# Moving the routing marks to GpSimd and reordering the routing inside a fused attention and mixture-of-experts kernel

## The chip, the cores and the metric

The kernel runs on one core of a Trainium2 chip. The metric is the device time of one execution in microseconds (us). The core's engines run side by side, each through its own queue in the order in which it was written: TensorE (PE in the profile; PEld is its weight load), VectorE (DVE), ScalarE (ACT), GpSimd (POOL) and SyncE (SP, which only issues transfers). Semaphores tie them together.

## The reference, cut to what matters

Sliding-window attention (4 batches, 8 heads, 576 positions, width 64, window 64) gives 2304 tokens of 512 columns. A router with noise picks two of eight experts for each token and weighs them; each expert is two matrix products with a ReLU between. The sum goes through a last feed-forward block (2048 columns, a piecewise quadratic gate).

```python
scores = np.where((rel >= 0) & (rel < 64), q @ k.T / 8, -1e9)
x = softmax(scores) @ v                               # 2304 x 512
noisy = x @ w_gate + np.log1p(np.exp(x @ w_noise)) * noise
top2, top2_w = two largest of noisy, softmax over the two
out[t] = sum over the two: top2_w * (np.maximum(x[t] @ w1[e], 0) @ w2[e])
return gate(out @ w_in) @ w_out                       # w_in, w_out come as float64
```

## The kernel before

**Stages.** The first stage is attention, in half-steps `step(u)`, u = 0 to 36. A tile is 128 tokens; two half-steps, an even and an odd one, carry one tile through a pipeline of several tiles at once. An even step does the scores of the tile ahead (`A`, L282 and L291), transposes an older output tile (`Ex`, L347), transposes probabilities (`C`, L313), and multiplies them with the values (`Dm`, L327). An odd step has `C` and the router's logits (`logits`, `Gm`, L365). ScalarE does the exponentials (L306) and copies out of PSUM (L315, L349); VectorE does the maxima (L298), the normalised values (L332, L333, L335) and copies the logits (L368). GpSimd scales the maxima (L299) and copies 64 value rows per tile (L340) that the next tile's `Dm` reads.

**Routing.** The 18 tiles form three groups of six (`GROUPS`). When a group's last logits are there, `route(g)` is made, a generator. Every step calls `advance(marks)`, which lets it go on to its next `yield` of 1 or 2 (`yield 0` does not stop it), and then lets up to `marks` queued calls run. In order, the generator computes the noisy logits, the two largest and their indices (L454, L457), one-hot rows and their sums (L460 to L478), then the positions of the tokens within their experts as matrix products (L482 to L486), their split in row and column (L491 to L505), and queues 12 calls (6 tiles, 2 choices), each `mark_r` and `mark_e`. A mark is a 128x128 (`ohr`, L510) or 128x145 (`ohe`, L517, for odd tiles of a group; L520 on ScalarE for even ones) matrix in 16 bits, comparing a row of numbers with a token's position. `place()` multiplies each pair of marks on TensorE (L557, "products of marks") and so scatters token numbers into the ids of the experts' lists. Marks made in one step are multiplied in the next.

**Early part of expert 0.** When groups 0 and 1 (24 products) are placed, `early()` copies the ids (L385), computes the first 384 tokens of expert 0 and gathers them through GpSimd's queue (L650, three transfers, tiles `xg0a`). They are transposed (L672) in steps 35 and 36, and unit `0a` (expert 0, three blocks of 128 tokens) starts at once (L763 first products, L803 second ones, with values split in a high and a low part). Group 2 is routed during `0a` by `tail()`, which ends with the full ids, the gathers of the rest of expert 0 (`0b`, L745) and of expert 1's first blocks (`xge`, L745). L792 scatters results, also by GpSimd. Then come experts 1 to 7 and the last block.

**Weights.** A chunk of 128 hidden columns is loaded as float32 (L134) and split into a high part (ScalarE, L147) and a low part (VectorE, L148). `EW` chunks are loaded and split, half by half, during attention, one every `LS` steps from step `L0`; `F0` is where splits go on inside unit `0a`. `MARKS` is the number of queued calls per step (before and after the last ten steps of attention), `TAIL` the same in `tail()`.

Of the kernel before, what the change touches and what calls it, by code (L numbers as in the profile page):

```python
# [18 lines left out]
ALU = mybir.AluOpType  # L19
AX = mybir.AxisListType  # L20

P = 128
# [6 lines left out]
NT = N // P  # L29
# [6 lines left out]
GROUPS = [6, 6, 6]  # L36
EARLY = 2
NA = 3
MARKS, TAIL = (2, 6), 6
Y0, LOOK = 3, 1  # L40
PTB = 3
EW, L0, LS, F0 = 10, 1, 3, 4
G2 = [2, 4, 4, 4, 4]
NCE = E * NF
MID = N // 2
# [8 lines left out]
def fused_kernel(ctx, tc, qT, kT, v, wg, noise, wcat, out, wd=None):  # L54
    nc = tc.nc
# [16 lines left out]
    att, rte, ffn = ExitStack(), ExitStack(), ExitStack()  # L72
    wk = rte.enter_context(tc.tile_pool(name="wk", bufs=2, side="right"))
    gp = rte.enter_context(tc.tile_pool(name="gp", bufs=2, side="right"))
    oh = rte.enter_context(tc.tile_pool(name="oh", bufs=8, side="right"))
    ac = rte.enter_context(tc.tile_pool(name="ac", bufs=1, side="right"))
    qk = att.enter_context(tc.tile_pool(name="qk", bufs=2))
    vp = att.enter_context(tc.tile_pool(name="vp", bufs=4))
# [125 lines left out]
    for s in (0, 64):  # L204
        nc.gpsimd.affine_select(out=id64[s:s + 64, :], in_=id64[s:s + 64, :], compare_op=ALU.not_equal, fill=1.0,
                                base=0, pattern=[[-1, 64]], channel_multiplier=1)
        m = m0[s:s + 64]
# [4 lines left out]
    for c, k in ((0, 1), (0, 0), (1, 1)):  # L212
        for h in range(2):
            o = masks[c][k][:, 64 * h:64 * h + 64]
# [19 lines left out]
    io145 = ac.tile([P, NK], F16, name="io145")  # L234
# [67 lines left out]
    def soft(u):  # L302
        sb, nb = Sb[u % 3], mxs.pop(u)
        p = wk.tile([P, 4, P], F32, tag="p", name=f"p{u}", bufs=4)
        for g in range(4):
            nc.scalar.activation(p[:, g, :], sb[:, g * P:g * P + P], AF.Exp, bias=nb[:, g:g + 1], scale=0.125)  # L306
        pr[u] = p
# [106 lines left out]
    def route(g):  # L414
# [40 lines left out]
        yield calm  # L455
        for a in range(T):
            nc.vector.max_index(out=ix[:, a, :], in_max=mx8[:, t0 + a, :], in_values=ny[:, a, :])  # L457
        yield calm
        ixf = tl("ixf", [P, T, 2])
        nc.vector.tensor_copy(ixf, ix[:, :, 0:2])  # L460
        yield 0
# [45 lines left out]
        def mark_r(a, c):  # L507
            o = oh.tile([P, P], F16, tag="ohr", name=f"ohr{g}_{a}_{c}")
            code = tcode2 if a % 2 else tcode
            nc.vector.tensor_scalar(out=o, in0=io145[:, 1:P + 1], scalar1=rf[:, a, 0, c:c + 1],  # L510
                                    scalar2=code[:, t0 + a:t0 + a + 1], op0=ALU.is_equal, op1=ALU.mult)
            rows[g, a, c] = o

        def mark_e(a, c):
            ej = oh.tile([P, NK], F16, tag="ohe", name=f"ohe{g}_{a}_{c}")
            if a % 2:
                nc.vector.tensor_scalar(out=ej, in0=io145, scalar1=rf[:, a, 1, c:c + 1], scalar2=0.0, op0=ALU.add,  # L517
                                        op1=ALU.is_ge)
            else:
                nc.scalar.activation(ej, io145, AF.Sign, bias=rf[:, a, 1, c:c + 1])  # L520
            pq.append((c, rows.pop((g, a, c)), ej))
# [29 lines left out]
    def place():  # L551
        while pq:
            c, o, ej = pq.popleft()
            if nids[0] == n_early:
                open_ids()
            nids[0] += 1
            nc.tensor.matmul(IDS2[:, c, :], lhsT=o, rhs=ej, start=False, stop=(nids[0] in (n_early, 2 * NT)))  # L557
# [34 lines left out]
    def logits(i, u):  # L592
        Gm(i, u)
        g, t = tile_group[i]
        if t == GROUPS[g] - 1:
            live.append(route(g))
            next(live[-1])

    def step(u):
        for c in range(EW):  # L600
            if u == L0 + LS * c:
                load_raw(c)
        if u + 2 < NU:
            if (u + 2) % 4 == 0 and (u + 2) // 4 + 1 < NT // 2:
                load_qk((u + 2) // 4 + 1)
                keys_before((u + 2) // 4 + 1)
            if (u + 1) % 2 == 0 and (u + 1) // 2 + 1 < NT:
                load_v((u + 1) // 2 + 1)


        m = u // 2
        if u % 2 == 0:
            if u + 2 < NU:
                A(m + 1)
            if 0 <= m - 2 < NT:
                Ex(m - 2, u)
        if u < NU:
            C(u)
        if u % 2 == 0 and u + 2 < NU:
            top(u + 2)  # L620
            top(u + 3)
        if u + 2 < NU:
            soft(u + 2)
        place()
        early()
        if 0 <= u - 1 < NU:
            Dm(u - 1)
        if u % 2 == 1 and 0 <= m - 2 < NT:
            logits(m - 2, u)
        advance(MARKS[u > NU - 10])  # L630

        for c in range(EW):
            for h in range(2):
                if u == L0 + LS * c + 3 + h:
                    split_w(c, h)
            if u == L0 + LS * c + 4 and c >= EW - 2:
                load_raw(c + 2)
# [57 lines left out]
    def tail():  # L695
        logits(NT - 2, NU + 1)
        Ex(NT - 1, NU + 1)
        advance(TAIL)
        yield
        logits(NT - 1, NU + 1)  # L700
        while live or oq or pq:
            place()
            advance(TAIL)
            yield
        finish_ids([(NA, NB), (0, NA), (NB, E * JB)])
        count()
        rte.close()
        pool["xp"] = ffn.enter_context(tc.tile_pool(name="xp", bufs=2, reuse_waits="tile", side="right"))
        for b in range(units[1]["nb"]):
            prep_gather(units[1], b)  # L710
            yield

    def count():
        cnt = bank[6][:, CNT:CNT + E]
# [248 lines left out]
    for s in range(len(seq)):  # L963
# [26 lines left out]
        else:  # L990
            ahead = [(nxt, b, b + lag) for b in range(nxt["nb"])] if ui and ui not in (SPILL, U7A) and nxt else []
        for x, b, w in ahead:
            if f == w:
                prep_gather(x, b)

        def ahead_xpose():
# [76 lines left out]
```

## Time and profile before

| | us |
|---|---|
| median of 3 runs (lowest, highest) | 1016.88 (1015.85, 1021.69) |
| the profiled execution | 1017.2 |
| its span, first to last instruction | 1015.5 |
| TensorE busy | 987.3 (97%) |
| VectorE, ScalarE, GpSimd busy | 573.8, 417.7, 197.7 |
| first product of unit 0a (L763) starts at | 123.03 |

The profile is one execution. Its page gives each engine's busy time, the span in 40 slices with TensorE's granted clock, and the costliest groups of instructions; the trace behind it answers by stretch, by line and by wait. TensorE is busy nearly throughout, so a time of another engine counts only where TensorE waits for it, and a busy TensorE at half its clock does half the work. In the granted clock 1.00 is 2.4 GHz and 0.50 is 1.2 GHz.

### The profile page before, as it was taken

The page shows a single profiled execution, that of the slowest core. Times are in us where ns is not written, and L with a number is a line of the kernel's source. Part 1 is how long each engine was busy: PE and PEld are TensorE (multiplying, and loading weights), DVE is VectorE, ACT ScalarE, POOL GpSimd, SP SyncE. Part 2 cuts the span into 40 slices and gives each one's busy share as a digit, 9 for nine tenths or more (in the row PEclk, how much of TensorE's full clock was granted, in tenths as well). Part 3 has the DMA queues.
Part 4 walks back from the last instruction along what each step waited for, and adds up shares of the span by engine and source line. Part 5 has one row for each costly group of instructions (what it writes and reads, how often), then busy time and mean ns, then how long its engine had stood idle before and what let it go on. Part 6 is the DMA issues. An engine that isn't in the chain of part 4 may idle for free.

```text
span 1015.5 us, 16345 instructions
## 1 busy us (share of the span) xinstructions
PE 987.3 (97%) x6373; PEld 853.9 (84%) x6374; DVE 573.8 (57%) x1112; ACT 417.7 (41%) x811; POOL 197.7 (19%) x257
## 2 busy tenths in 40 slices
PE   8987899999999999999999999999999999999998
PEld 5876778999999999999987999888888888888886
DVE  4687465567675757665443656645445544545443
ACT  6886424444444544443334544424223322422221
POOL 3221103223324343432312111102001000200000
PEclk9998799999999999999999999999999999999999
DMA  8875305556666666677433643020020002001001
GB/s 253 283 238 188 105 21 183 180 178 192 211 210 199 205 203 202 189 219 258 139 102 121 219 148 92 21 83 22 0 104 21 1 1 105 21 1 41 1 1 42
DMA packets 50048, 127.01 MB, mean 125 GB/s; under 512 B 5296, under 2 KB 15792, under 8 KB 49968
## 3 DMA queue, kind: packets, MB, share of 16 engines
q1 hardware_dynamic: 39616, 93.94, 30.1%
q0 software_dynamic: 9056, 29.63, 7.8%
q10 hardware_dynamic: 1296, 2.36, 0.6%
q8 instruction: 51, 0.84, 0.3%
q14 instruction: 29, 0.24, 0.1%
HBM read 97.47 MB, written 28.44 MB: 124 GB/s over the span
## 4 chain that ended last, share of the span: by engine, by line
PE 86%; DVE 1%; DMA 0%; POOL 0%; ACT 0%; issue 0%; another core or an unknown queue 0%; POOLq 0%; ACTq 0%
PE bank L763 42%; PE bank L803 41%; PE bank L672 2%; PE bank L830 1%; DMA xge<-x_dram,src_i 0%; PE bank L841 0%; PE bank L365 0%; PE ob L327 0%; POOL y_dram L792 0%; POOL xg0a L650 0%; PE bank L347 0%; DVE hl0a L770 0%; PE bank L557 0%; PE bank L313 0%; ACT hh0a L769 0%
## 5 line engine op out<-in xcount | busy, mean ns | idle before, releaser
L803 PE MATMUL bank<-w,hhg 128*128 128x512 f32 x576 | 178.2, 390 | 0.0
L803 PE MATMUL bank<-w,hhe 128*128 128x512 f32 x480 | 151.0, 396 | 0.0
L763 PE MATMUL bank<-xhig,w 128*128 128x512 f32 (+1 forms) x640 | 149.2, 375 | 0.0
L763 PEld LDWEIGHTS bank<-xhig,w 128*128 128x128 f32 x640 | 112.4, 188 | 22.5
L148 DVE TENSOR_TENSOR w<-raw,w 128x1024 fp32r<-128x1024 f32 (+1 forms) x90 | 99.5, 1106 | 52.0 <-ACT w L147 49.0
L763 PE MATMUL bank<-xhie,w 128*128 128x320 f32 x768 | 128.5, 309 | 0.0
L803 PEld LDWEIGHTS bank<-w,hhg 128*128 128x128 f32 x576 | 107.2, 188 | 23.1
L763 PEld LDWEIGHTS bank<-xhie,w 128*128 128x128 f32 x768 | 118.7, 188 | 3.8
L803 PE MATMUL bank<-w,hlg 128*128 128x512 f32 x288 | 112.4, 390 | 0.0
L779 DVE TENSOR_SCALAR m<-r 128x512 f32<-128x512 f32 (+1 forms) x80 | 32.2, 402 | 130.1 <-ACT r L776 130.0
L782 ACT ACTIVATE hhg<-r 128x512 fp32r<-128x512 f32 (+1 forms) x80 | 47.2, 590 | 134.8 <-DVE r L781 130.5
L776 ACT ACTIVATE r<-bank 128x512 f32<-128x512 f32 (+1 forms) x80 | 44.5, 556 | 140.9 <-PE bank L763 140.8
L770 DVE SCALAR_TENSOR_TENSOR hle<-bank,hhe 128x320 fp32r<-128x320 f32 x96 | 47.0, 490 | 98.1 <-ACT hhe L769 95.6
L803 PEld LDWEIGHTS bank<-w,hhe 128*128 128x128 f32 x480 | 87.1, 188 | 15.6
L803 PE MATMUL bank<-w,hle 128*128 128x512 f32 x240 | 93.7, 391 | 0.0
L769 ACT ACTIVATE hhe<-bank 128x320 fp32r<-128x320 f32 x96 | 41.8, 436 | 125.1 <-PE bank L763 117.2
L147 ACT ACTIVATE w<-raw 128x1024 fp32r<-128x1024 f32 (+1 forms) x90 | 87.3, 971 | 13.2 <-PE bank L803 10.8
L783 DVE TENSOR_TENSOR hlg<-r,hhg 128x512 fp32r<-128x512 f32 (+1 forms) x80 | 56.1, 702 | 58.8 <-ACT hhg L782 58.8
L763 PE MATMUL bank<-xlog,w 128*128 128x512 f32 (+1 forms) x320 | 80.5, 373 | 0.0
L891 POOL TENSOR_TENSOR y<-y 128x512 f32<-128x512 f32 x16 | 25.7, 1605 | 247.0 <-ACT y L890 245.5
L763 PE MATMUL bank<-xloe,w 128*128 128x320 f32 x384 | 71.9, 309 | 0.0
L183 POOL TENSOR_TENSOR dt<-rawd 128x512 f32<-128x512 f32 x32 | 33.2, 1037 | 175.7 <-DVE rawd L181 159.7
(244 smaller groups left out, 1491.7 us busy)
## 6 DMA issues: line engine op xcount, KB each, us to landing
raw<-wcat SPq DMA_DIRECT2D x64, 512.0 KB, 4.2
rawd<-wd SPq DMA_DIRECT2D x32, 512.0 KB, 4.5
w2f<-dt POOLq DMA_DIRECT2D x32, 256.0 KB
raw<-w2f SPq DMA_DIRECT2D x16, 512.0 KB, 3.5
y<-y_dram SPq DMA_DIRECT2D x16, 512.0 KB, 4.7
vE<-v SPq DMA_DIRECT2D x18, 260.0 KB, 4.5
x_dram<-x SPq DMA_DIRECT2D x18, 256.0 KB, 2.4
k<-kT SPq DMA_DIRECT2D x8, 512.0 KB, 6.4
```

Of the source, the lines that this page charges most:

```text
L147: nc.scalar.activation(w[:, 0, c], t[:, c], AF.Copy)
L148: nc.vector.tensor_tensor(out=w[:, 1, c], in0=t[:, c], in1=w[:, 0, c].bitcast(F32), op=ALU.subtract)
L183: nc.gpsimd.tensor_tensor(out=t.bitcast(F32), in0=hf, in1=lf, op=ALU.add)
L763: nc.tensor.matmul(ps, lhsT=l[:, k * P:k * P + P], rhs=r[:, k, s:s + w], start=(c == 0), stop=(c == len(prods) - 1))
L769: nc.scalar.activation(hh, ps, AF.Relu)
L770: nc.vector.scalar_tensor_tensor(out=hl, in0=ps, scalar=0.0, in1=hh.bitcast(F32), op0=ALU.max, op1=ALU.subtract)
L776: nc.scalar.activation(r, ps, AF.Relu, bias=1.0)
L779: nc.vector.tensor_scalar(out=m, in0=r, scalar1=0.5, scalar2=1.0, op0=ALU.mult, op1=ALU.min)
L782: nc.scalar.activation(hh, r, AF.Copy)
L783: nc.vector.tensor_tensor(out=hl, in0=r, in1=hh.bitcast(F32), op=ALU.subtract)
L803: nc.tensor.matmul(M2[b], lhsT=l[:, sl], rhs=r[n], start=(first and a == 0), stop=(last and a == 2))
L891: nc.gpsimd.tensor_tensor(out=y2, in0=y2, in1=y1, op=ALU.add)
```

## The change

There are six edits. In an odd step the logits come ahead of the products of marks. `advance()` is called ahead of `Dm`, so VectorE has the routing ahead of the values. The marks of VectorE (all L510 and the L517) are issued on GpSimd. `route` stops once more, after the indices of the two largest (`yield 2`), and fewer calls run per step in the last ten steps and in `tail()` (four instead of six); marks have ten buffers instead of eight. Eight chunks instead of ten are split during attention, one every four steps, and the splits in `0a` start at its third chunk. Expert 1's first block is gathered at the end of `tail()`.

```diff
-MARKS, TAIL = (2, 6), 6
+MARKS, TAIL = (2, 4), 4
...
-EW, L0, LS, F0 = 10, 1, 3, 4
+EW, L0, LS, F0 = 8, 1, 4, 2
...
-    oh = rte.enter_context(tc.tile_pool(name="oh", bufs=8, side="right"))
+    oh = rte.enter_context(tc.tile_pool(name="oh", bufs=10, side="right"))
...
             nc.vector.max_index(out=ix[:, a, :], in_max=mx8[:, t0 + a, :], in_values=ny[:, a, :])
-        yield calm
+        yield 2
...
-            nc.vector.tensor_scalar(out=o, in0=io145[:, 1:P + 1], scalar1=rf[:, a, 0, c:c + 1],
+            nc.gpsimd.tensor_scalar(out=o, in0=io145[:, 1:P + 1], scalar1=rf[:, a, 0, c:c + 1],
                                     scalar2=code[:, t0 + a:t0 + a + 1], op0=ALU.is_equal, op1=ALU.mult)
...
             if a % 2:
-                nc.vector.tensor_scalar(out=ej, in0=io145, scalar1=rf[:, a, 1, c:c + 1], scalar2=0.0, op0=ALU.add,
+                nc.gpsimd.tensor_scalar(out=ej, in0=io145, scalar1=rf[:, a, 1, c:c + 1], scalar2=0.0, op0=ALU.add,
                                         op1=ALU.is_ge)
...
         if u + 2 < NU:
             soft(u + 2)
+
+        if u % 2 == 1 and 0 <= m - 2 < NT:
+            logits(m - 2, u)
         place()
         early()
+        advance(MARKS[u > NU - 10])
         if 0 <= u - 1 < NU:
             Dm(u - 1)
-        if u % 2 == 1 and 0 <= m - 2 < NT:
-            logits(m - 2, u)
-        advance(MARKS[u > NU - 10])
...
         for b in range(units[1]["nb"]):
             prep_gather(units[1], b)
             yield
+        prep_gather(units[2], 0)
...
         for x, b, w in ahead:
-            if f == w:
+            if f == w and (x["key"], b) not in gat:
                 prep_gather(x, b)
```

GpSimd's queue from a tile of group 0, before: scalings of two maxima (`nb24`, `nb25`, L299), the copy of value rows (`vE10`), the same for the next tile, and the copy of keys (`k8`, L109).

```order
L299 TENSOR_SCALAR nb24_1325<-mx24_1324 128x4
L299 TENSOR_SCALAR nb25_1329<-mx25_1328 128x4
L340 COPY vE10_1028<-vE11_1135 64x520
L299 TENSOR_SCALAR nb26_1436<-mx26_1435 128x4
L299 TENSOR_SCALAR nb27_1440<-mx27_1439 128x4
L340 COPY vE11_1135<-vE12_1242 64x520
L109 COPY k8_1514<-k7_1288 128x4x64
```

The same place after.

```order
L299 TENSOR_SCALAR nb24_1316<-mx24_1315 128x4
L299 TENSOR_SCALAR nb25_1320<-mx25_1319 128x4
L510 TENSOR_SCALAR ohr0_1_0_1330<-io145_178,rf0_1266,tcode2_183 128x128
L517 TENSOR_SCALAR ohe0_1_0_1332<-io145_178,rf0_1266 128x145
L510 TENSOR_SCALAR ohr0_1_1_1334<-io145_178,rf0_1266,tcode2_183 128x128
L517 TENSOR_SCALAR ohe0_1_1_1336<-io145_178,rf0_1266 128x145
L340 COPY vE10_1021<-vE11_1126 64x520
L510 TENSOR_SCALAR ohr0_2_0_1381<-io145_178,rf0_1266,tcode_180 128x128
L510 TENSOR_SCALAR ohr0_2_1_1385<-io145_178,rf0_1266,tcode_180 128x128
```

The four marks of tile 1 of the group stand behind the two scalings and ahead of the copy of value rows; two more follow in the odd step.

TensorE's queue in that odd step, before: transposes of probabilities (`p23`), two products of marks with their weight loads, logits of tile 9.

```order
L313 MATMUL bank3_75<-idn_163,p23_1250 128x128 x4
L557 LDWEIGHTS ohr0_1_0_1362
L557 MATMUL bank7_77<-ohe0_1_0_1364,ohr0_1_0_1362 128x145
L557 LDWEIGHTS ohr0_1_1_1366
L557 MATMUL bank7_77<-ohe0_1_1_1368,ohr0_1_1_1366 128x145
L365 MATMUL bank5_76<-wg_sb_127,xt9_1316 128x16 x4
```

After.

```order
L313 MATMUL bank3_75<-idn_163,p23_1241 128x128 x4
L365 MATMUL bank5_76<-wg_sb_127,xt9_1307 128x16 x4
L557 LDWEIGHTS ohr0_1_0_1330
L557 MATMUL bank7_77<-ohe0_1_0_1332,ohr0_1_0_1330 128x145
L557 LDWEIGHTS ohr0_1_1_1334
L557 MATMUL bank7_77<-ohe0_1_1_1336,ohr0_1_1_1334 128x145
```

The logits now stand between the transposes and the products.

GpSimd's queue at the early gathers, before: `xg0a` are the gathers, `vE15` and `vE16` the last two copies of value rows.

```order
L340 COPY vE14_1483<-vE15_1598 64x520
L299 TENSOR_SCALAR nb34_1950<-mx34_1949 128x4
L299 TENSOR_SCALAR nb35_1954<-mx35_1953 128x4
L650 DMA xg0a_0_1974<-x_dram_68,src_i_189 128x512
L650 DMA xg0a_1_1976<-x_dram_68,src_i_189 128x512
L650 DMA xg0a_2_1978<-x_dram_68,src_i_189 128x512
L340 COPY vE15_1598<-vE16_1710 64x520
L340 COPY vE16_1710<-vE17_1866 64x520
```

After, from the last mark of tile 3 of group 1 on.

```order
L517 TENSOR_SCALAR ohe1_3_1_1925<-io145_178,rf1_1843 128x145
L340 COPY vE15_1584<-vE16_1696 64x520
L510 TENSOR_SCALAR ohr1_4_0_1973<-io145_178,rf1_1843,tcode_180 128x128
L510 TENSOR_SCALAR ohr1_4_1_1977<-io145_178,rf1_1843,tcode_180 128x128
L510 TENSOR_SCALAR ohr1_5_0_1981<-io145_178,rf1_1843,tcode2_183 128x128
L517 TENSOR_SCALAR ohe1_5_0_1983<-io145_178,rf1_1843 128x145
L510 TENSOR_SCALAR ohr1_5_1_1985<-io145_178,rf1_1843,tcode2_183 128x128
L517 TENSOR_SCALAR ohe1_5_1_1987<-io145_178,rf1_1843 128x145
L651 DMA xg0a_0_2015<-x_dram_68,src_i_189 128x512
L651 DMA xg0a_1_2017<-x_dram_68,src_i_189 128x512
L651 DMA xg0a_2_2019<-x_dram_68,src_i_189 128x512
L340 COPY vE16_1696<-vE17_1810 64x520
```

The gathers stand two steps later, behind the last six marks of group 1; one of the two copies is now ahead of them, the other still behind.

## Rows read from the trace of the kernel before

**Rows 1.** Waits of TensorE, 57 to 180 us: us in total, times, longest.
```profile
PE bank L557 <- DVE ohr L510: 4.6, 2, 4.1
PE bank L557 <- DVE ohe L517: 3.9, 7, 1.1
PE ob L327 <- POOL vE L340: 2.2, 1, 2.2
PE bank L672 <- DMA xge<-x_dram,src_i: 1.4, 1, 1.4
PE bank L482 <- DVE ohs L467: 1.3, 2, 1.1
PE bank L482 <- ACT pt L315: 1.2, 1, 1.2
PE bank L763 <- DVE xlo0a L676: 1.1, 1, 1.1
PE bank L313 <- DVE lgs L368: 0.6, 1, 0.6
```

**Rows 2.** Stretches: us; busy PE PEld DVE ACT POOL; clock; DMA share; GB/s.
```profile
63.65:67.06 3.41, 3.41 (x40) 2.79 (x32) 2.66 (x11) 1.94 (x5) 0.44 (x2) 0.50 0.86 269
...
77.31:80.72 3.41, 3.41 (x43) 2.85 (x43) 1.82 (x5) 0.60 (x2) 0.00 (x0) 0.50 0.84 268
...
97.78:108.02 10.24, 8.24 (x70) 6.76 (x72) 7.21 (x31) 5.67 (x17) 0.55 (x3) 0.50 0.16 53
...
114.85:121.68 6.83, 6.83 (x61) 6.38 (x60) 2.62 (x8) 1.91 (x4) 0.61 (x1) 0.50 0.21 77
```

**Rows 3.** Timeline of TensorE, an odd step: start, us, what, idle before and releaser.
```profile
69.56 0.22 PE L557 MATMUL bank<-ohe,ohr 128*128 128x145 f16 x1 [1.07 <-DVE ohe L517]
```

**Rows 4.** Timeline of TensorE, one tile at 2.4 GHz: first row of each part.
```profile
85.63 0.41 PE L282 MATMUL bank<-mask,id 64*64 64x512 bf16 x4
...
87.87 1.15 PE L327 MATMUL ob<-vE,pt 128*64 128x65 f32 x32
88.95 0.66 PE L313 MATMUL bank<-idn,p 128*128 128x128 f32 x4
89.45 0.96 PE L365 MATMUL bank<-wg_sb,xt 128*128 128x16 f32 x8
90.34 0.41 PE L282 MATMUL bank<-mask,id 64*64 64x512 bf16 x4
```

**Rows 5.** Groups by line and shape: count, busy us, mean ns, idle before.
```profile
L340 POOL COPY vE<-vE 64x520 f32<-64x520 f32 x17 | 10.4, 613 | 6.0 <-POOL nb L299 3.3 <-issue 2.6
L299 POOL TENSOR_SCALAR nb<-mx 128x4 f32<-128x4 f32 x36 | 8.0, 222 | 74.3 <-DVE mx L298 69.1 <-ACT L L433 2.6 <-DVE rl L332 2.2
...
L244 POOL TENSOR_SCALAR tcode<-tcode 128x18 f32<-128x18 f32 x1 | 0.3, 302 | 0.1
L225 POOL CAST idr<-idn 128x128 fp32r<-128x128 f32 x1 | 0.3, 296 | 0.0
```

**Rows 6.** Groups by line of VectorE, 60 to 150 us, columns as in rows 5.
```profile
L510 DVE TENSOR_SCALAR ohr<-io,rf,tcode 128x128 f16<-128x128 f16 x36 | 10.0, 314 | 0.0
```

**Rows 7.** Timeline of VectorE, group 1's indices.
```profile
97.91 0.25 DVE L491 TENSOR_TENSOR o<-o,bank 128x96 f32<-128x96 f32 x1
...
98.97 0.17 DVE L505 TENSOR_SCALAR rf<-ri 128x12 f32<-128x12 int32 x1
```

**Rows 8.** Timeline, the early ids: VectorE's copy, GpSimd's first gather.
```profile
107.78 0.46 DVE L385 COPY first<-bank 128x290 f32<-128x290 f32 x1 [0.92 <-PE bank L557]
...
109.34 1.21 POOL L650 DMA_INDIRECT xg0a<-x_dram,src_i  x1 [2.10 <-DVE rl L332]
```

**Rows 9.** Timeline of GpSimd, the issue of unit 0b's second gather.
```profile
149.47 0.99 POOL L745 DMA_INDIRECT xg0b<-x_dram,src_i  x1 [0.30 <-issue]
```

**Rows 10.** Sums of a stretch, columns as in rows 2.
```profile
149.80:152.70 2.90, 2.90 (x16) 2.51 (x15) 2.66 (x15) 1.44 (x2) 0.66 (x1) 1.00 0.61 181
```

**Rows 11.** Groups by line: TensorE's second products of unit 0a.
```profile
L803 PE MATMUL bank<-w,hh0a 128*128 128x512 f32 x48 | 15.2, 397 | 0.0
```

## The prediction

> **What bounds the kernel now.** I first took the list of TensorE's waits, then the stretches of granted clock, then the timelines around the longest waits. From 160 us on the list holds one wait (1.4 us, on the first gather of expert 1) and little else, so nothing after about 180 us has idle time that this change could remove. What can move lies between 60 and 180 us: the end of attention, where the routing of token groups 0 and 1 is woven in, and expert 0, where group 2 is routed. The waits there [rows 1] are, with L482 the positions and L557 the products of marks: 1.2 and 1.3 us for positions, 4.6 and 3.9 us for marks, 2.2 us for values behind the early gathers, 1.1 us for the first gathered tokens, 0.6 us for logits. They come to 14.9 us, of which 13.1 lie before expert 0's first product (at 123.03); the other 1.8 are group 2's, 1.1 for positions and 0.7 for marks.
>
> Idle time is half of it. TensorE's clock was granted at 0.50, that is 1.2 GHz, in four stretches, 23.9 us in all, with 3.41 + 3.41 + 8.24 + 6.83 = 21.9 us of busy TensorE [rows 2]; shortly before each of them TensorE had stood idle (the 1.2 for positions, one of the 1.1 for marks, the 4.1 and the 2.2 of [rows 1], in this order). At 2.4 GHz this work takes half, so the low clock costs some 10.9 us. Together 13.1 + 10.9 = 24 us. That is the most that could be won there, and I expect under half of it.
>
> **The change part by part.**
>
> *Products a step behind; logits first.* In an odd step TensorE does four transposes and then waits for marks that VectorE makes after the values of the pair: 1.07 us [rows 3] and a little for the second, three times alike: 3.7 of the 3.9 us in [rows 1]. Now the logits stand ahead of the products. They are there anyway and take 0.89 us at full clock (from 89.45 to 90.34 [rows 4]), so marks as late as today's would leave some 0.3 us of each 1.2. Cost nothing; if the marks come later than that, the rest returns.
>
> *Marks by GpSimd.* 54 operations leave VectorE (36 of L510, 18 of L517) and join GpSimd's queue, two in an odd step of group 0, four in an even one, and six in a step of groups 1 and 2. No row shows this form on GpSimd. Lower bound: the cast of 128x128 on GpSimd, 0.296 us [rows 5]. Upper bound: the two tensor_scalars there, 0.222 us at 4 columns and 0.302 at 18, make 5.7 ns a column, and at 128 columns 0.93 us; but the 18-column one is a single, first instruction of its kind. The copy of 520 columns takes 0.613. I take 0.40 us: the cast, which has the mark's size, and a third more for the second operation.
> The Trainium skill speaks against this part: GPSIMD Engine Reference, section Engine selection, sends elementwise work to VectorE and puts GpSimd at about twice its time for two inputs, near line rate for one. By it the sum would be 1014 (the rival below); the cast's row speaks for the lower price, and no run here shows the form itself.
>
> In group 0 the four marks of an even step follow the two scalings of the maxima. Those follow the scores by some 1.75 us, so the marks are ready at 1.75 + 4 x 0.40 = 3.35 us after the scores. TensorE reaches the products later: from the start of a tile to its end 4.71 us [rows 4], less 1.28 for the scores, 3.4 us. It just fits. GpSimd's work of a tile, 6 x 0.40 + 2 x 0.22 + 0.61 + some 0.2 of key copy, is 3.7 us, under the tile's. Behind the marks waits only the copy of value rows, needed a tile later. The first such tile is worse: the second half of a weight split now waits, through ScalarE, for the marks' positions, and the maxima stand behind it on VectorE; I count 1.5 us once. Positions of group 0 come out of a bank that ScalarE must first empty, which the reordering helps only because a split is further ahead: 0.6 of 1.2 us stays. So 1.2 + 3.7 becomes 0.6 + 1.5, and the split's wait is where it would cost more: with the marks any later, every tile has it.
>
> *Routing ahead of the values, spread further.* The 4.1 us wait [rows 1] is group 1's positions and marks run as one chain behind maxima and values. Now the positions come a step later and the twelve marks take three steps of four instead of two of six. I count from the end of the positions (0). From L491 to the end of L505 it is 1.2 us [rows 7], so with the way to VectorE the indices are there at 1.45; six marks end at 1.45 + 2.4 = 3.85, where TensorE comes at 2.24 (scores, transposes [rows 4]): 1.6 us idle. Two scalings (0.44) and six marks more: 6.7, TensorE at 6.5: 0.2. Value copy 0.61 and six marks: 9.7, TensorE at 8.2: 1.5. In a formula: 2.7 + 18 x price = 9.9. So the early part's 5.0 us (4.1, 0.1, 0.2 and the 0.6 for logits) becomes 3.3.
>
> *Early gathers two steps later.* They start when group 1's last product is done. Today that was 15 us before expert 0, now it is about 9. From the products' end to the first issue took 1.6 us (the copy at 107.78 follows the products at once, the issue stands at 109.34 [rows 8], with L385 starting 0.1 after the last product). Landing: of two gathers the second was issued at 149.47 and the 0.52 MB of both had moved by 152.70 [rows 9, 10], 3.2 us; I take 3.4 for the first. That is 5.0 us, while TensorE has 1.08 + 0.50 + 0.89 = 2.5 us of work: 2.5 idle. The last value copy stands behind the three issues (3.7 us) as today's did, 0.5 more. So 2.2 becomes 3.0. This part loses.
>
> *The clock.* The idle pieces left are smaller but lie close: 1.5 in the first mark tile, 1.6, 1.5 and 2.5 at the end. I expect a fall after the first, one after the second, and one of double length at the end, 13.6 us with some 10 us of busy TensorE, hence 5.0 lost instead of 10.9.
>
> *Expert 0.* Group 2's positions lose their 1.1 us (a product of weights stands between). Its 0.7 us for marks becomes max(6p - 1.45, 12p - 3.8, 18p - 6.6), with p the price of a mark: GpSimd's 6, 12 or 18 marks from 3.9 us on, against TensorE's products, which ask for them after 5.35, 7.7 and 10.5 us (six products of 0.397 [rows 11], 2.4 us, and a little more between them). At 0.40 it is 1.0. The first gather of expert 1, now issued ahead of the three scatters, gives back its 1.4. Two splits (four halves of 0.69 on VectorE) go from attention to expert 0, under its products; TensorE sees them only where VectorE makes it wait, which the formula's 3.9 start of the indices there already holds (2.7 with the split, 1.2 for the steps of [rows 7]).
>
> **Sum**, against the profiled execution's 1017.2 us (span 1015.5; the median of the runs, 1016.88, is 0.3 lower, so it needs no shift): idle before expert 0 from 13.1 to 0.6 + 1.5 + 3.3 + 3.0 + 1.1 (first gathered tokens, unchanged) = 9.5, that is -3.6; clock -5.9; positions and marks of group 2 -0.8; gather -1.4. Together -11.7, of which I give back 0.7 because sums of single durations leave no room for jitter between engines: 1006.
>
> **Rivals.**
> *The marks cost 0.63 us*, twice VectorE's 0.314 [rows 6]. Group 1's chain: 18 x 0.23 = +4.1; group 2: 4.7 instead of 1.0, +3.7: 1014. For it: the two tensor_scalar rows rise with width faster than the copies; against: the cast's row. It is what the page of the Trainium skill named above would make of it.
> *GpSimd becomes the bound (slower).* Each 0.1 us of price costs 3.6 us in the two chains, so at 0.40 + 11 / 36 = 0.71 us a mark the gain is gone, and above some 0.68 GpSimd's queue is also longer than a tile in group 0 (0.93: 6 x 0.93 + 1.25 = 6.8 against 5.35 with products, three tiles, +4.2). At 0.93: +9.5 + 9 + 4.2 = 1029. For it: the upper bound; against: it rests on one first instruction.
> *The clock stays low as long as today* (10.9 lost): 1006 + 5.9 = 1012. For it: the waits I leave are of the size that preceded the falls.
> *Cheap marks*, 0.30: 18 x 0.1 less in the chain, group 2 at 0.4, a fall less: 1001.
> *Nothing moves*: the waits just go to the gathers, whose landing takes 5 us or more in a busy stretch: 1016.
>
> **How the numbers follow.** Forecast (1002 to 1010) 0.50; cheap marks 0.12; clock 0.14, half of it on each side of the bound; 0.63 us a mark 0.13; slower 0.08; nothing 0.03. A half per cent, 5 us, is what a measurement of this kernel can tell from no change: faster under 1011.8, slower over 1022. Faster 0.50 + 0.12 + 0.07 = 0.69, same 0.07 + 0.13 + 0.03 = 0.23, slower 0.08. 1000 to 1016 leaves out the slower case and the tail of cheap marks, under 2 in 10.
>
> **What would show it.** After: L510 and L517 on GpSimd at 0.35 to 0.45 us; no wait over 0.4 at L557 in the odd steps of group 0 but the first; the 4.1 us wait gone, two of about 1.5 in its place; a wait of 2 to 3 us of TensorE on the early gather (L651); none at expert 1's first transposes; expert 0's first product at 112 to 114 us; half-clock time before it of 10 to 17 us instead of 23.9. A mark at 0.6 or more, or a clock low for over 20 us, would make me wrong upwards; marks so early that TensorE never waits for them, downwards.

## The result and the profile after

| | before | after |
|---|---|---|
| median (lowest, highest), 20 runs each, us | 1018.2 (1012.33, 1024.43) | 1025.41 (1021.97, 1032.49) |
| profiled execution's span, us | 1015.5 | 1023.6 |
| GpSimd busy, us | 197.7 | 242.1 |
| first product of expert 0 (L763, now L765) at, us | 123.03 | 127.50 |

After is slower: ratio 1.0076 of the time before, 95% interval 1.0057 to 1.0094. The forecast was 1006 us in a range of 1000 to 1016. Line numbers behind L631 are one or two higher in the kernel after (L650 is L651, L672 is L673, L763 is L765).

The price of a mark, by line (minimum, median and maximum ns of one, then the starts of first and last):

```profile
L510 POOL TENSOR_SCALAR ohr<-io,rf,tcode x36: 783/800/1462, 64.8 to 159.6; 128x128 f16<-128x128 f16 x36
L517 POOL TENSOR_SCALAR ohe<-io,rf x18: 785/793/819, 69.2 to 160.4; 128x145 f16<-128x145 f16 x18
```

It is 0.80 us where the forecast had 0.40 and VectorE had taken 0.314 [rows 6]. TensorE's waits between 57 and 190 us (total, times, longest; two of 0.6 us left out), which answer to [rows 1]:

```profile
PE bank L557 <- POOL ohe L517: 14.7, 14, 2.0
PE bank L557 <- POOL ohr L510: 1.9, 5, 0.6
PE bank L482 <- ACT pt L315: 1.5, 2, 1.2
PE bank L765 <- DVE xlo0a L677: 1.0, 1, 1.0
```

The waits on VectorE's marks (4.6 and 3.9), on the values (2.2) and on expert 1's gather (1.4) are gone. In their place TensorE waits 16.6 us for GpSimd's marks. And its clock, stretch by stretch (start and end, length, busy TensorE with its instructions, granted clock, DMA share, GB/s), to be held against [rows 2]:

```profile
56.50:72.22 15.72, 12.37 (x211) 1.00 0.84 280
72.22:75.63 3.41, 3.41 (x42) 0.50 0.08 26
75.63:85.87 10.24, 8.01 (x139) 1.00 0.68 222
85.87:89.28 3.41, 3.32 (x41) 0.50 0.31 113
89.28:99.52 10.24, 9.02 (x177) 1.00 0.46 156
99.52:126.83 27.31, 20.65 (x181) 0.50 0.29 88
126.83:150.72 23.89, 20.32 (x118) 1.00 0.18 56
150.72:157.55 6.83, 5.59 (x17) 0.50 0.28 77
```

At 0.50 (1.2 GHz) TensorE worked 3.41 + 3.32 + 20.65 + 5.59 = 33.0 us, before it was 21.9. The one long stretch is the whole of group 1's marks, from its positions to expert 0; TensorE was idle for a quarter of it.

The loss by place comes from cutting both traces at the same work: from the logits of the ninth tile (which both reach undisturbed) to expert 0's first product, and from there to expert 1's. First the kernel before, then the one after:

```profile
60.46:123.03 62.57, 49.42 (x678) 0.81 0.47 154
123.03:188.73 65.70, 62.27 (x376) 1.00 0.38 118
```

```profile
61.58:127.50 65.92, 51.70 (x677) 0.74 0.44 143
127.50:198.46 70.96, 64.69 (x376) 0.95 0.40 124
```

Length less busy is idle: 13.2 and 3.4 us before, 14.2 and 6.3 after. Half of the work done at half clock is what the clock cost: 10.9 and 0 before, 13.7 and 2.8 after. Together 27.5 before, 37.0 after, 9.5 us more. After also starts the stretch 1.1 us later, and has no fall of the clock near 541 us, which cost the execution before 1.7 us. That makes 8.9; the span grew by 8.1.

### The profile page after: what moved, and what is told of

Same layout as the page of the kernel before. It is cut to its first block, busy times and chain, and to the rows that moved or that the text cites. A ratio compares the mean times of both kernels' runs of the same rounds, so it can differ in the third digit from the quotient of the medians.

```text
span 1023.6 us, 16346 instructions
## 1 busy us (share of the span) xinstructions
PE 990.5 (97%) x6373; PEld 857.3 (84%) x6374; DVE 563.8 (55%) x1056; ACT 417.6 (41%) x809; POOL 242.1 (24%) x311
## 4 chain that ended last, share of the span: by engine, by line
PE 82%; ACT 0%; issue 0%
PE bank L765 40%; PE bank L805 39%; PE bank L673 2%; PE bank L832 1%; PE bank L843 0%; ACT hh L835 0%; ACT yg L810 0%; PE bank L823 0%
## 5 line engine op out<-in xcount | busy, mean ns | idle before, releaser
L765 PE MATMUL bank<-xhig,w 128*128 128x512 f32 (+1 forms) x640 | 149.1, 375 | 0.0
L765 PEld LDWEIGHTS bank<-xhig,w 128*128 128x128 f32 x640 | 112.4, 188 | 22.5
L765 PE MATMUL bank<-xhie,w 128*128 128x320 f32 x768 | 128.5, 309 | 0.0
L765 PEld LDWEIGHTS bank<-xhie,w 128*128 128x128 f32 x768 | 118.7, 188 | 3.7
L147 ACT ACTIVATE w<-raw 128x1024 fp32r<-128x1024 f32 (+1 forms) x88 | 86.7, 987 | 12.6 <-PE bank L805 10.8
L765 PE MATMUL bank<-xlog,w 128*128 128x512 f32 (+1 forms) x320 | 80.5, 373 | 0.0
L765 PE MATMUL bank<-xloe,w 128*128 128x320 f32 x384 | 71.9, 309 | 0.0
```

What stands on the lines that cost most here:

```text
L147: nc.scalar.activation(w[:, 0, c], t[:, c], AF.Copy)
L765: nc.tensor.matmul(ps, lhsT=l[:, k * P:k * P + P], rhs=r[:, k, s:s + w], start=(c == 0), stop=(c == len(prods) - 1))
```

## The experiments

Theory 1: the marks' price on GpSimd is the loss, and everything else in the change gains. Rivals: the other edits lose (order, splits, gathers), or GpSimd is the wrong place whatever a mark costs. Each run is compared with runs of the kernel before on the same chip, whose median was 1017.7 for the first four runs, 1017.1 for the next four, 1013.3 for the three behind them and 1012.4 for the last; so ratios are what compares across them.

### Marks back on VectorE

```diff
-            nc.gpsimd.tensor_scalar(out=o, in0=io145[:, 1:P + 1], scalar1=rf[:, a, 0, c:c + 1],
+            nc.vector.tensor_scalar(out=o, in0=io145[:, 1:P + 1], scalar1=rf[:, a, 0, c:c + 1],
...
-                nc.gpsimd.tensor_scalar(out=ej, in0=io145, scalar1=rf[:, a, 1, c:c + 1], scalar2=0.0, op0=ALU.add,
+                nc.vector.tensor_scalar(out=ej, in0=io145, scalar1=rf[:, a, 1, c:c + 1], scalar2=0.0, op0=ALU.add,
```

> The changed kernel with the marks (L510, L517) back on VectorE; its order, pacing, splits and the early gather of expert 1 stay. Theory 1 (the price of a mark on GpSimd, 0.80 us, and the low clock that follows it are the whole loss): 18 marks of a group take 5 us on VectorE instead of 14, no wait at L557 over 1 us, half-clock time under 15 us; 1005 to 1010 us beside a kernel before of 1017 to 1018, ratio 0.987 to 0.993. Theory 2 (four marks a step and early gathers two steps later are the loss, the marks' price is hidden): 1020 to 1025, ratio over 1.003, with TensorE waiting at the early gathers.

Measured 1003.71 us (1000.43 to 1006.70), ratio 0.9858 [0.9828, 0.9888]: theory 1, and a little faster than it had it. The five other edits gain 1.4%, and the move of the marks costs 1025.4 - 1003.7 = 22 us on top of them. The same cut of its trace:

```profile
62.00:112.24 50.24, 41.73 (x677) 0.95 0.58 190
112.24:178.36 66.12, 65.76 (x376) 0.93 0.44 132
```

Idle 8.5 and 0.4 us. TensorE's waits there show what the reordering turned into: the early gathers, now nearer to their use, as forecast.

```profile
PE bank L673 <- DMA xg0a<-x_dram,src_i: 2.3, 2, 2.0
PE bank L482 <- ACT pt L315: 1.6, 2, 1.3
PE bank L557 <- DVE ohe L517: 1.4, 5, 0.5
PE bank L535 <- DVE first L385: 1.1, 1, 1.1
```

### The move of the marks alone

```diff
-            nc.vector.tensor_scalar(out=o, in0=io145[:, 1:P + 1], scalar1=rf[:, a, 0, c:c + 1],
+            nc.gpsimd.tensor_scalar(out=o, in0=io145[:, 1:P + 1], scalar1=rf[:, a, 0, c:c + 1],
...
-                nc.vector.tensor_scalar(out=ej, in0=io145, scalar1=rf[:, a, 1, c:c + 1], scalar2=0.0, op0=ALU.add,
+                nc.gpsimd.tensor_scalar(out=ej, in0=io145, scalar1=rf[:, a, 1, c:c + 1], scalar2=0.0, op0=ALU.add,
```

> The kernel before with the marks on GpSimd and nothing else. Theory 1: six marks a step need 9 operations of 0.80 us on GpSimd where the chain needs them at once, twice for group 1 and twice for group 2, and one tile of group 0 has 6 x 0.80 + 1.25 = 6 us on GpSimd; 1024 to 1032 us, ratio 1.006 to 1.014, as slow as the changed kernel or slower. Theory 2: the marks' price is hidden, 1015 to 1020, ratio 0.998 to 1.002.

Measured 1043.78 us (1041.27 to 1047.39), ratio 1.0262 [1.0232, 1.0293], worse than any theory had it. In the kernel before's own order TensorE waits for marks in every odd step and for group 1's in one piece:

```profile
PE bank L557 <- POOL ohe L517: 19.3, 14, 2.1
PE bank L557 <- POOL ohr L510: 8.7, 9, 4.5
```

So the move alone costs 26 us, and the rest of the change wins back 18 of them.

### Prices on GpSimd

Thirty-two operations at the end of the kernel before, on scratch tiles, each form four times. They lengthen the run, so its time (1041.04 us) says nothing; the rows do.

```diff
+        nc.gpsimd.tensor_scalar(out=po[:, 0:128], in0=pf[:, 0:128], scalar1=s1, scalar2=s2, op0=ALU.is_equal, op1=ALU.mult)
+        nc.gpsimd.tensor_scalar(out=po[:, 0:64], in0=pf[:, 0:64], scalar1=s1, scalar2=s2, op0=ALU.is_equal, op1=ALU.mult)
+        nc.gpsimd.tensor_scalar(out=po, in0=pf, scalar1=s1, scalar2=s2, op0=ALU.is_equal, op1=ALU.mult)
+        nc.gpsimd.tensor_scalar(out=po[:, 0:128], in0=pf[:, 0:128], scalar1=3.0, scalar2=None, op0=ALU.mult)
+        nc.gpsimd.tensor_scalar(out=po[:, 0:128], in0=pf[:, 0:128], scalar1=s1, scalar2=None, op0=ALU.is_equal)
+        nc.gpsimd.tensor_scalar(out=po[:, 0:128], in0=pf[:, 0:128], scalar1=3.0, scalar2=4.0, op0=ALU.add, op1=ALU.mult)
...
+        nc.gpsimd.tensor_copy(po[:, 0:128], pf[:, 0:128])
```

> The kernel before with 32 extra operations on GpSimd at its very end, eight forms four times each, on scratch tiles: the mark (128x128, 16 bits, two operations with a column of scalars each), the same at 64 and 256 columns, one operation with a constant, one with a column, two with constants, two with columns on 32 bits, and a copy. If the price goes by columns for every tensor_scalar (the line through 0.222 at 4 and 0.302 at 18 columns): 0.55, 0.93, 1.66 us at 64, 128, 256 columns for all forms alike. If two operations or a column of scalars make it: 0.8 for those, 0.3 to 0.4 for one with a constant. If company of VectorE made it: 0.4 for all, since VectorE uses little of the memory beside them here. The time itself is not a question; the operations lie beside TensorE's last products.

One line a form, in the order of the diff (minimum, median, maximum ns):

```profile
L1049 POOL TENSOR_SCALAR pb<-pa x4: 790/791/824, 1005.7 to 1023.1; 128x128 f16<-128x128 f16 x4
L1050 POOL TENSOR_SCALAR pb<-pa x4: 577/577/827, 1006.6 to 1024.0; 128x64 f16<-128x64 f16 x4
L1051 POOL TENSOR_SCALAR pb<-pa x4: 1217/1217/1220, 1007.5 to 1024.7; 128x256 f16<-128x256 f16 x4
L1052 POOL TENSOR_SCALAR pb<-pa x4: 537/537/545, 1008.8 to 1026.0; 128x128 f16<-128x128 f16 x4
L1053 POOL TENSOR_SCALAR pb<-pa x4: 597/600/601, 1009.5 to 1026.6; 128x128 f16<-128x128 f16 x4
L1054 POOL TENSOR_SCALAR pb<-pa x4: 297/297/297, 1010.1 to 1027.3; 128x128 f16<-128x128 f16 x4
L1056 POOL COPY pb<-pa x4: 289/290/291, 1011.3 to 1028.4; 128x128 f16<-128x128 f16 x4
```

A mark costs 0.79 us on an otherwise idle GpSimd too, so VectorE's company doesn't make its price: 0.36 us, and 3.3 ns for each column (64, 128 and 256 columns lie on one line). In 32 bits it took 0.796. What makes it dear is its form, not its size: at the same 128x128 a compare and a multiply with two columns of scalars took 0.791, a compare with one column 0.600, a multiply by one constant 0.537, and an add and a multiply with two constants 0.297, as much as a copy. The operations, their number and the kind of scalars change together from form to form, so which of them sets the price is not shown. My estimate from the cast had the size right and the kind wrong.

### The two reorderings alone

The kernel before, with the logits ahead of the products and `advance()` ahead of `Dm`.

```diff
+        if u % 2 == 1 and 0 <= m - 2 < NT:
+            logits(m - 2, u)
         place()
         early()
+        advance(MARKS[u > NU - 10])
         if 0 <= u - 1 < NU:
             Dm(u - 1)
-        if u % 2 == 1 and 0 <= m - 2 < NT:
-            logits(m - 2, u)
-        advance(MARKS[u > NU - 10])
```

> The kernel before with only the two reorderings: logits ahead of the products of marks, and the routing ahead of the values; marks on VectorE, six a step at the end. Theory 1: the three waits of 1.07 + 0.17 us in group 0 go, with the fall of the clock near 77 us, 4 to 6 us in all; 1011 to 1014, ratio 0.994 to 0.996. Theory 2 (order does not matter, the waits move to the values): 1016 to 1020, ratio 0.998 to 1.002.

Measured 1009.32 us (1005.27 to 1011.87), ratio 0.9914 [0.9886, 0.9942], somewhat more gain than theory 1 had. The order is worth 0.9% of the 1.4%; the longest wait for marks fell from 4.1 to 0.7 us. What it leaves: 3.6 us of waits for positions, 1.8 for the values and 1.3 for expert 1's gather.

### Which of the small edits gain

Three variants of the changed kernel with its marks on VectorE (1003.71 us, 0.9858). The first has six calls a step again.

```diff
-MARKS, TAIL = (2, 4), 4
+MARKS, TAIL = (2, 6), 6
```

> The changed kernel with its marks back on VectorE (1003.7 us) and, besides, six queued calls per step instead of four (MARKS 2, 6 and TAIL 6). Theory A, the spread serves any engine that makes the marks: six marks of 0.31 with maxima and values behind them are late again, a wait of 0.7 us or more at the products and at the values, 1005 to 1008. Theory B, the spread was only needed for a mark of 0.8 us: with VectorE one step less of marks brings the early gathers forward, the 2.0 us wait on them goes, 1000 to 1002.

1001.1 us (1000.42 to 1002.43), 0.9851 [0.9828, 0.9873]: in time not told apart from four calls. Its trace has no wait on the early gathers, as theory B said; a wait of 1.9 us for the counts (L535) stands instead. It is the fastest median of all.

The second has the splits of before.

```diff
-EW, L0, LS, F0 = 8, 1, 4, 2
+EW, L0, LS, F0 = 10, 1, 3, 4
```

> The changed kernel with its marks back on VectorE (1003.7 us), with the splits of before: ten chunks early, one every three steps, from the fourth chunk on in unit 0a. Theory A, most of what the rest of the change gains beyond the two reorderings (1009.3 to 1003.7) is the thinner splits, since VectorE has two splits less where group 0 is placed: 1006 to 1008. Theory B, splits are covered either way: 1003 to 1005.

1005.68 us (1002.99 to 1006.44), 0.9888 [0.9863, 0.9912]. Between the two expectations, and the intervals overlap: 2 us perhaps, not settled.

The third gathers expert 1's first block in its turn again.

```diff
-        prep_gather(units[2], 0)
```

> The changed kernel with its marks back on VectorE (1003.7 us), without the gather of expert 1's first block ahead of time. Theory A, the prediction's term: the wait of 1.3 to 1.4 us at expert 1's first transposes is back, 1005. Theory B, the gather does not matter, since the queue is late anyway: no change, 1003.7.

1003.07 us (1000.35 to 1006.22), 0.9870 [0.9841, 0.9899]. The wait came back as theory A said, yet no time can be told apart; one microsecond is less than these runs resolve.

```profile
PE bank L673 <- DMA xge<-x_dram,src_i: 1.1, 1, 1.1
```

### A third of the marks on GpSimd

The changed kernel with L510 on VectorE; only L517 (18 of 54) stays.

```diff
-            nc.gpsimd.tensor_scalar(out=o, in0=io145[:, 1:P + 1], scalar1=rf[:, a, 0, c:c + 1],
+            nc.vector.tensor_scalar(out=o, in0=io145[:, 1:P + 1], scalar1=rf[:, a, 0, c:c + 1],
```

> The changed kernel with L510 back on VectorE and only L517 (18 of 54 marks) left on GpSimd. Theory A, the price counts only where marks stand in one row: at most two of 0.8 us now fall into a step, beside VectorE's, which fits under TensorE's work: 1002 to 1006, like VectorE alone. Theory B, GpSimd's marks cost also by slowing VectorE when both run: a third of the loss, 1008 to 1012.

1008.65 us (1004.05 to 1009.41), 0.9908 [0.9878, 0.9938]. By its time theory B, by its trace A: between the ninth tile and expert 1 it has 8.5 + 0.7 us of idle time against 8.5 + 0.4 with all marks on VectorE, and the marks of VectorE keep their median of 306 ns. Its profiled span is 1.9 us longer, 1.65 of which lie ahead of the ninth tile, where no mark is made. Which it is stays open.

### The price as the only difference

Four runs of the changed kernel: in three, GpSimd makes every mark in a form of another price; the third in order is their control, with the price as it was. In all four the row marks (L510) are zero, so the lists of the experts are empty; each slot reads one and the same token row and, by one more changed line (not shown), writes a row of its own. The last block waits 1.8 us less in them (0.5 instead of 2.3 us at L843), so they stand against the control. L517 is changed like L510 in the other three (not shown). The first form has two constants and a broadcast input:

```diff
-            nc.gpsimd.tensor_scalar(out=o, in0=io145[:, 1:P + 1], scalar1=rf[:, a, 0, c:c + 1],
-                                    scalar2=code[:, t0 + a:t0 + a + 1], op0=ALU.is_equal, op1=ALU.mult)
+            nc.gpsimd.tensor_scalar(out=o, in0=rf[:, a, 1, c:c + 1].to_broadcast([P, P]), scalar1=0.0,
+                                    scalar2=0.0, op0=ALU.is_equal, op1=ALU.mult)
```

> The changed kernel with every GpSimd mark in a cheap form: two constants instead of the column scalars, the token's position read as a broadcast input so that the wait on it stays. The marks are all zero, so the lists are empty; every expert reads the same token row and writes rows of its own, the amount of work is as before. Theory A, the prediction's formula holds and only its price was wrong: at some 0.30 us a mark the time is 1001 (the prediction's case of cheap marks), 999 to 1005. Theory B, marks on GpSimd cost by their place (the way from VectorE, the copies and the gathers behind them), whatever one costs: 1010 or more.

1016.9 us (1013.85 to 1018.03), 1.0036 [1.0018, 1.0054]. The form wasn't cheap:

```profile
L510 POOL TENSOR_SCALAR ohr<-rf x36: 630/640/1018, 66.4 to 153.9; 128x128 f16<-128x128 f32 x36
```

L517 took 0.72. So it is a point at 0.67, not at 0.30. Its input is one 32-bit column read over and over, and its first operation is a compare; which of the two makes it dear is not shown.

The second has one column of scalars and one operation:

```diff
+            nc.gpsimd.tensor_scalar(out=o, in0=io145[:, 1:P + 1], scalar1=rf[:, a, 1, c:c + 1],
+                                    scalar2=None, op0=ALU.is_equal)
```

> The same with one column scalar and one operation a mark, 0.60 us; marks all zero as well. Theory A, the prediction's formula: 36 x 0.20 = 7.2 us over its forecast of 1006 at 0.40, so 1013, 1010 to 1016. Theory B, place alone: the same as with the cheap form.

1015.67 us (1013.25 to 1018.18), 1.0025 [1.0009, 1.0041], at 0.60 and 0.66 us a mark:

```profile
L510 POOL TENSOR_SCALAR ohr<-io,rf x36: 590/600/1148, 64.6 to 154.0; 128x128 f16<-128x128 f16 x36
```

The control compares with a number that never matches:

```diff
-            nc.gpsimd.tensor_scalar(out=o, in0=io145[:, 1:P + 1], scalar1=rf[:, a, 0, c:c + 1],
+            nc.gpsimd.tensor_scalar(out=o, in0=io145[:, 1:P + 1], scalar1=rf[:, a, 1, c:c + 1],
```

> Control: the changed kernel with its own form and price of a mark (0.80 us), but L510 compared with a number that never matches, so that its marks are zero as in the two runs beside it. Theory A: like the changed kernel, 1022 to 1028, since the content of the marks sets no time. Theory B: if empty lists alone make the kernel faster, under 1018, and the two runs beside it are to be read against this one.

1022.53 us (1021.01 to 1023.51), 1.0095 [1.0075, 1.0115]: like the changed kernel, so empty lists alone make nothing faster that matters here. Its price, its waits for marks, its two stretches and the two longest at half clock:

```profile
L510 POOL TENSOR_SCALAR ohr<-io,rf,tcode x36: 781/794/1389, 65.1 to 160.0; 128x128 f16<-128x128 f16 x36
PE bank L557 <- POOL ohe L517: 14.2, 12, 1.9
PE bank L557 <- POOL ohr L510: 1.9, 4, 0.7
61.78:127.94 66.16, 50.81 (x677) 0.77 0.46 143
127.94:198.32 70.38, 64.72 (x376) 0.95 0.43 125
103.44:127.33 23.89, 17.65 (x155) 0.50 0.30 79
151.22:158.05 6.83, 5.69 (x17) 0.50 0.28 77
```

The last form reads, with two constants, a 16-bit tile of which VectorE writes one column a group:

```diff
+        nc.vector.tensor_copy(wd16[:, 0:1], rf[:, T - 1, 1, 1:2])
...
+            nc.gpsimd.tensor_scalar(out=o, in0=wd16[:, 0:P], scalar1=3.0,
+                                    scalar2=0.0, op0=ALU.add, op1=ALU.mult)
```

> The cheap mark once more, since the broadcast input of the run before cost 0.64 and 0.72 us and not 0.30: now GpSimd reads a 16-bit tile with two constants (0.30 us in the table of prices), and one small copy a group on VectorE carries the wait on the positions. Marks all zero, lists empty, as in the three runs before. Theory A, the price alone: by the prediction's formula 1001 at 0.30 us; the three runs before lay 2 to 5 us above the formula, so 1002 to 1007, 0.985 to 0.990 of the kernel before. Theory B, GpSimd's place costs whatever a mark does: 1010 or more, 0.993 and up.

1004.43 us (1001.45 to 1006.42), 0.9925 [0.9897, 0.9954]. Theory A by the microseconds; the ratio lies between the two, since the runs of before were 4 to 5 us faster than those the formula was written for. Prices, waits and stretches of its trace, and its two stretches at half clock (its lines are four higher from L510 on):

```profile
L514 POOL TENSOR_SCALAR ohr<-wd x36: 288/295/1257, 63.5 to 137.9; 128x128 f16<-128x128 f16 x36
L521 POOL TENSOR_SCALAR ohe<-wd x18: 310/317/319, 67.0 to 138.2; 128x145 f16<-128x145 f16 x18
```

```profile
PE bank L677 <- DMA xg0a<-x_dram,src_i: 3.3, 3, 2.6
PE bank L561 <- POOL ohe L521: 2.6, 8, 0.6
```

```profile
60.00:111.80 51.80, 41.90 (x677) 0.97 0.60 185
111.80:177.01 65.21, 63.66 (x376) 0.97 0.47 132
105.68:109.09 3.41, 3.33 (x40) 0.50 0.82 140
112.50:115.92 3.42, 3.42 (x14) 0.50 0.34 131
```

Little but the price differs between this kernel and its control, and with it go 13.1 of the control's 16.1 us of waits for GpSimd's marks and most of the time at half clock. The four points lie near one line:

| mean price of a mark, us (L510, L517) | group 1: end of positions to end of its last mark, us (2.7 + 18 x price) | idle in the two stretches, us | lost to the clock there, us | time, us | ratio |
|---|---|---|---|---|---|
| 0.30 (0.295, 0.317) | 8.5 (8.1) | 9.9 + 1.5 | 3.4 | 1004.4 | 0.9925 |
| 0.62 (0.600, 0.657) | 14.9 (13.9) | 12.0 + 3.9 | 16.1 | 1015.7 | 1.0025 |
| 0.67 (0.640, 0.722) | 15.3 (14.7) | 14.1 + 3.7 | 10.8 | 1016.9 | 1.0036 |
| 0.79 (0.794, 0.788) | 17.7 (17.0) | 15.4 + 5.7 | 15.1 | 1022.5 | 1.0095 |

From 0.30 to 0.79 it is 18.1 us, 37 us for each us of price; the forecast had 36. By the ratios, since the first row ran on another chip than the rest, it is 17 us and 35.

The price is not shown to be all. Held against the run with the marks on VectorE (0.9858), where they took 0.31 and 0.26 us, the kernel with marks of 0.30 on GpSimd (0.9925) is 0.7% slower by the ratios, and the intervals don't overlap; by the microseconds it is 0.7 us, on two chips. Its trace has 2.6 us more idle time in the two stretches. So of the 22 us of the move some 17 are the price's, and up to 7 may belong to the place or to the chips.

In the changed kernel itself the row of positions and the first and the last marks read as follows (start, length, engine, line), 98.65 to 116.29, 17.6 us:

```profile
98.38 0.27 PE L486 MATMUL bank<-ohs,ones 128*128 128x40 bf16 x5
...
100.68 2.37 POOL L510 TENSOR_SCALAR ohr<-io,rf,tcode 128x128 f16<-128x128 f16 x3 [2.84 <-DVE rf L505]
...
115.50 0.79 POOL L517 TENSOR_SCALAR ohe<-io,rf 128x145 f16<-128x145 f16 x1
```

## Why the prediction was wrong

**The step that failed is a size: "I take 0.40 us".** It measured 0.80. My bounds, 0.296 and 0.93, held it. The choice between them went by the mark's size (the cast), where it should have gone by its kind: the two tensor_scalars [rows 5], 0.222 at 4 columns and 0.302 at 18, already rose far faster than the copies. Nor were they of the mark's kind: both (L299, L244) multiply 32-bit numbers by one constant, and with a constant 128 columns took 0.537. No row of the kernel before had a column of scalars on GpSimd. The rule of the Trainium skill that I weighed there (GPSIMD Engine Reference, section Engine selection) pointed the right way and not far enough: about twice VectorE's time would be 0.63, and against VectorE's 0.314 the mark took 2.5 times. The page has near line rate for one input, and doesn't say whether a mark, with one tensor and two columns of scalars, counts as one input or two. What came true is the rival "GpSimd becomes the bound", with its break-even at 0.71 and 1029 at 0.93, to which I gave 0.08; the runs at 0.62 and 0.67 came out 0.3% above the time of before, the one at 0.79 1.0%. Between 0.30 and 0.62 a straight line of the ratios crosses 1 at 0.54 us (my estimate), so the break-even came earlier than I had it.

**The chain was right.** 2.7 + 18 x price for group 1 came within 0.4 to 1.0 us at four prices and in the changed kernel (17.6, by the formula 17.1). Its parts make 2.5 and not 2.7 (1.45 + 0.44 + 0.61); by that it was 0.6 to 1.2 short.

**The slope was right, its working not.** I had it as 18 + 18 marks of idle time for TensorE and the clock as a term by itself. With 0.80 in place of 0.40 my own terms give 1022: 7.2 us more for group 1, 6.8 for group 2 and 2.1 for group 0 (three tiles of 6 x 0.80 + 1.25 against 5.35). With the right price I would thus have forecast a slower kernel, but with 26.8 us of idle time where 20.5 were measured, and 5.0 lost to the clock where it was 16.5. In the table idle time takes 11.4 to 21.1 us, some 20 us for each us of price; the clock's loss grows from 3.4 to 15.1, and not evenly (16.1 at 0.62, 10.8 at 0.67). Both are of single executions, and the one profiled at 0.30 was the fastest of its seven, at a mean granted clock of 0.997 where the others had 0.986 to 0.993, so there 3.4 is rather the least. I read it so: while a chain lasts, TensorE has its other work to do, so less of the chain is idle time; but much of that work is done at half clock. The two errors cancel in the slope, not in the forecast's terms:

| term, us | forecast | after | at a price of 0.30 |
|---|---|---|---|
| idle before expert 0 | 9.5 | 14.2 | 9.9 |
| idle in expert 0 (3.4 before, less 0.8 and 1.4) | 1.2 | 6.3 | 1.5 |
| lost to the clock | 5.0 | 16.5 | 3.4 |

The misses are 4.7 + 5.1 + 11.5 = 21.3. With the start (+1.1), the missing late fall (-1.7), the 0.7 that I had given back (-0.7) and some 0.8 us less of recorded work, this makes 19.2 of the 19.3 us between 1006 and the profiled execution's 1025.3.

**Point by point.** *Logits first*: the odd steps wait again, 2.2 and 2.1 us in two tiles of group 0, where 1.5 once was forecast; I had written that with dearer marks every tile would. *Routing ahead of the values*: the 4.1 us wait is gone, and 2.8, 0.3 and 2.5 us stand in its place instead of 1.6, 0.2 and 1.5. *Positions*: group 0's waited 0.3 us instead of 0.6, but group 1's 1.2 (1.3 with the marks on VectorE), for ScalarE's copy out of the bank, and for that I had nothing. *Early gathers*: 2.5 us of idle time forecast, none in the changed kernel, since TensorE at half clock comes to them late; 2.3 us with the marks on VectorE and 3.3 at a price of 0.30, so the term was right for the kernel I had in mind. *Gather of expert 1*: its wait is gone as forecast, and back (1.1 us) where the edit is undone. *Expert 0's first product* at 112 to 114: it came at 127.50, but at 112.24 on VectorE and 111.80 at 0.30. *Half clock*, 10 to 17 us before it: 34.1; I had named over 20 as what would make me wrong upwards, and the runs show that it hung on the price as well: at 0.30 it was 3.4 before expert 0.

**What stays open**: whether marks on GpSimd cost anything beyond their price (a third of them there ran 0.5% behind none, all of them at 0.30 us 0.7%), which part of a mark's form makes it dear, and how the 0.5% beyond the two reorderings divides among pacing, splits and gather. The version that beats both kernels is the change without its third edit: 0.9858 of before with four calls a step, 0.9851 with six.

## What to carry to other kernels

Before moving an operation to another engine, look for a row there of the same kind (its operations, its scalars, its inputs), not of the same size; where there is none, measure the form alone, since one wrong price multiplied by a chain of eighteen decided this case. Don't hold TensorE's clock fixed while a chain's price varies: here its loss was 3.4 us at a mark of 0.30 and 10.8 to 16.1 at 0.62 and more. And when several edits come as one, undo the one with the unmeasured price first: here it alone turned a gain of 1.4% into a loss.

## What the runs showed of the hardware

GpSimd's time for a tensor_scalar of the same 128x128 went from 0.297 us (two constants, add and multiply) to 0.791 (two columns of scalars, compare and multiply), and a multiply by one constant alone took 0.537, more than two operations with two; why, no run shows.

One kernel's executions differ by TensorE's clock: beside the runs at 0.62 us the kernel before took 1009.8 us at a mean granted clock of 0.993 and 1018.4 at 0.982. So a clock term read from one profile holds for that execution.

VectorE and GpSimd held each other up. In the changed kernel a VectorE product of two inputs that takes 0.21 us in its median took 0.67, and ended with the GpSimd copy that had begun just before it:

```profile
97.23 0.61 POOL L340 COPY vE<-vE 64x520 f32<-64x520 f32 x1
97.24 0.67 DVE L467 TENSOR_TENSOR ohs<-o 128x48 bf16<-128x48 f32 x1
```

And the other way round, a mark took 1.22 us where VectorE's low part of a weight had started first:

```profile
108.74 0.68 DVE L148 TENSOR_TENSOR w<-raw,w 128x512 fp32r<-128x512 f32 x1
108.88 1.22 POOL L510 TENSOR_SCALAR ohr<-io,rf,tcode 128x128 f16<-128x128 f16 x1
```

The Trainium skill (SBUF — State Buffer, section Who interferes with whom) says that a VectorE instruction with two inputs in SBUF and a GpSimd instruction that reads SBUF exclude each other, whoever comes first; the trace agrees, with 0.46 and 0.42 us of delay here for 0.60 and 0.54 us of overlap.
